# The dense part's first four products, parts of x and two weight conversions moved among the attention's last transposes

## The chip, the core and the metric

The kernel runs on one core of one Trainium2 chip. The metric is the device time of one execution in microseconds (us). The kernel before took 1040.09 us, the median of three runs (1038.75, 1040.09 and 1040.95).

## What is computed

Three parts follow each other. The attention keeps, in each row of scores, only those within `tau` of the row's largest, and its output, with the heads side by side, is the input x of the first feed-forward part, whose output is the input of the second.

```python
# q, k, v: (4, 8, 576, 64); tau = 0.02
scores = 1.0 / np.sqrt(64) * np.matmul(q, k.transpose(0, 1, 3, 2))
thresh = np.max(scores, axis=-1, keepdims=True) - tau
scores = np.where(scores >= thresh, scores, -1000000000.0)
scores = scores - np.max(scores, axis=-1, keepdims=True)
attn = np.exp(scores)
attn = attn / (np.sum(attn, axis=-1, keepdims=True) + 1e-09)
x = np.matmul(attn, v)             # then (2304, 512): rows batch and token
# first feed-forward part: w_in (512, 2048), w_out (2048, 512), alpha (2048,)
h = x @ w_in
g = np.maximum(h, 0.0) + alpha * np.minimum(h, 0.0)
x = g @ w_out
# second: w1, w2 (512, 1024), w3 (1024, 1024), w_out2 (1024, 512)
out = ((x @ w1) * (x @ w2) @ w3) @ w_out2
```

## The kernel before

**The attention** goes through 16 pairs of heads. A pair has nine score units (four chunks of 128 rows for each of two heads, and one chunk that holds the last 64 rows of both). Each unit runs through a row of steps with names that the kernel's table of turns uses, with the unit's number behind the letter:

- Q, scores on TensorE (PE, line 402) into one of three PSUM slots; R, row maximum on VectorE (DVE, L426); H, threshold (DVE, L429); E, exponential on ScalarE (ACT, L437); M, masking with the row sum (DVE, L451), after which the PSUM slot is free.
- G, a small guard on GpSimd (POOL, L462); I, reciprocal (DVE, L467); C, scaling of the row (POOL, L474).
- T, transposes of the scaled rows on PE (L491, in three groups of four or five per chunk); X, their eviction by ACT (L501 to L509).
- V, the product with v (PE, L518, one for each half of the rows) and Y, its eviction by ACT into `xT` (L531, L533).

Ahead of a pair stand the loads of q and k (a), their splits into a high and a low part on POOL (bq0hi, bq0lo and so on, L181 and L188) and their transposes (PE, L291). The order of all these steps is fixed by `turn_order`: it emits a step as soon as what it depends on has been emitted, in the order of `PER * P + AT[key]`, with P the pair and `AT` a table of numbers. Each engine then works through its own queue in that order, and so does SyncE (SP), which issues the DMAs. Between the pairs, the first 14 tiles of w_in are loaded and converted (w0 to w8).

**The first feed-forward part** (the dense part) computes `h = x @ w_in` in three passes: x and the weights are split into a high and a low part of about half the bits, and of the four products of parts three are made. For a tile of 512 tokens one h product is 12 matmuls of 128x512 (PE, L985, out `h`), 16 of them (f = 0 to 15) cover the 2048 columns. ACT and DVE make g from h (L1056, L1061), then split it into `gs` (L183, L188), and an acc product of 12 matmuls (L985, out `acc`) adds its part of `g @ w_out` in four PSUM banks. The numbers f of the acc products follow those of the h products some places behind. Before the first h product stand the splits of x: four high parts on ACT (L183, `x<-xT`) and four low parts on DVE (L188).

**The conversions.** w_out, and the last two tiles of w_in, come as 64-bit numbers. A tile of them is loaded by SP into one of two buffers `raw` (L794); ACT makes two parts of it (L196 `raw<-raw` and L202 `m<-raw`), DVE does three steps on one part (L207, L209, L213), POOL adds the two (L218, `m<-m,raw`), which frees the `raw` buffer for the next load. ACT and DVE make the high and low half of the weights from the sum (`wu`, L823 and L829). The low half needs `sign_sb`, which DVE makes in three instructions (L760 to L762).

The order of the dense part is set by `list_order`, a planner that goes by costs in the code and hands out the buffers (`raw` 2, `m` 3, `u` 2, `gs` 2, `h` 4 banks). It begins where the attention's list ends, and all attention buffers are closed between the two:

```python
        for o in turn_order(ops, slots):
            o.emit(*o.engines)
...
        att_ctx.close()
...
        for o in list_order(ops, slots, DENSE_TURN):
            o.emit(o.engine)
```

The second feed-forward part follows in the same list.

## Time and profile before

| what | value |
|---|---|
| median of three runs | 1040.09 us |
| the profiled execution | 1039.72 us |
| span of the profile (first to last instruction) | 1037.9 us |
| PE busy | 1014.1 us (98%) |
| VectorE busy | 751.6 us (72%) |
| ScalarE busy | 580.6 us (56%) |
| GpSimd busy | 340.1 us (33%) |
| mean granted clock of PE | 0.998 of full speed |
| last attention product with v begins | 303.64 us after the span's start |
| first h product, first acc product | 307.66 us, 317.57 us |
| first dense tile's last h product begins | 385.48 us |

Times within the span count from its first instruction. The profiled execution took 1.82 us more than its span, and 0.37 us less than the median of the runs. A row of a timeline has start, length, engine, line, operation, output and inputs, shapes and number of instructions; in brackets stand the idle time of the engine before it and what ended that. The end of a matmul is modelled and holds its latency, so a group's length is more than the distance to the next group.

### The profile page before, as it was taken

Reading aid. Unit: us, or ns where it says so; the run is one execution under the profiler, and the core shown is the slowest. Engines: PE = TensorE matmul, PEld = TensorE weight load, DVE = VectorE, ACT = ScalarE, POOL = GpSimd, SP = SyncE. Lnnn points to the kernel's source line nnn. Section 1 sums busy time; section 2 is a strip of 40 time slices with the busy share of each in tenths; the row PEclk is TensorE's granted clock in tenths of the full one; section 3 lists DMA queues with packets and bytes.
Section 4 is the critical chain, followed back from the end, with each engine's and each line's share of the span. In section 5 each row is a group of like instructions: output and inputs, shape, how many; then the busy total and the mean of one; then the engine's idle time right before and its main releaser. Section 6 shows DMA issues by size and latency. Waiting matters only on the chain.

```text
span 1037.9 us, 16931 instructions
## 1 busy us (share of the span) xinstructions
PE 1014.1 (98%) x5870; PEld 867.0 (84%) x5870; DVE 751.6 (72%) x1556; ACT 580.6 (56%) x1119; POOL 340.1 (33%) x469
## 2 busy tenths in 40 slices
PE   8999999999989999999999999999999999999997
PEld 6778777777858889988888888888899999999997
DVE  7999999999858787667656565638475587577554
ACT  5998989999865665544443344324143363345331
POOL 4888888888733232222211211103200000000000
PEclk9999999999999999999999999999999999999999
DMA  5353443435113333434524233512242233224201
GB/s 128 90 141 100 131 112 117 125 89 153 39 41 104 112 110 114 141 117 156 176 80 142 104 136 106 172 41 72 92 139 75 81 108 122 71 72 148 91 11 61
DMA packets 71445, 109.50 MB, mean 106 GB/s; under 512 B 14912, under 2 KB 43584, under 8 KB 71360
## 3 DMA queue, kind: packets, MB, share of 16 engines
q1 hardware_dynamic: 68992, 108.16, 33.3%
q8 instruction: 46, 0.75, 0.3%
q10 hardware_dynamic: 2368, 0.27, 0.2%
q14 instruction: 39, 0.32, 0.1%
HBM read 80.22 MB, written 18.35 MB: 95 GB/s over the span
## 4 chain that ended last, share of the span: by engine, by line
PE 87%; POOL 5%; issue 2%; DVE 2%; ACT 2%; DMA 1%; SPq 0%; POOLq 0%; ACTq 0%; DVEq 0%
PE h L985 25%; PE acc L985 24%; PE h L1341 17%; PE pv_ps L518 8%; PE pt_ps L491 5%; PE s_ps L402 5%; POOL p L474 3%; PE tr L291 2%; POOL ks L181 1%; POOL qs L181 1%; PE zero L352 1%; PE h L858 1%; DMA raw<-in_moe_w_dram 0%; POOL praw L474 0%; ACT qT L311 0%
## 5 line engine op out<-in xcount | busy, mean ns | idle before, releaser
L985 PE MATMUL h<-x,wa 128*128 128x512 f32 (+1 forms) x960 | 212.4, 371 | 1.1 <-ACT x L183 1.1
L985 PE MATMUL acc<-gs,wu 128*128 128x512 f32 (+1 forms) x960 | 209.8, 368 | 0.4 <-DVE wu L829 0.4
L985 PEld LDWEIGHTS h<-x,wa 128*128 128x128 f32 x960 | 167.3, 189 | 32.6 <-ACT x L183 3.0
L985 PEld LDWEIGHTS acc<-gs,wu 128*128 128x128 f32 x960 | 168.1, 189 | 31.0 <-DVE wu L829 0.8
L1341 PE MATMUL h<-T,sw 128*128 128x384 f32 x1008 | 190.6, 336 | 0.0
L1341 PEld LDWEIGHTS h<-T,sw 128*128 128x128 f32 x1008 | 178.4, 188 | 8.3
L218 POOL TENSOR_TENSOR m<-m,raw 128x512 int32<-128x512 int32 x58 | 81.6, 1408 | 281.5 <-DVE m L213 213.9
L1405 DVE TENSOR_TENSOR ct<-h,ct 128x384 f32<-128x384 f32 x120 | 66.8, 557 | 91.6 <-PE h L1341 91.5
L426 DVE TENSOR_REDUCE sm<-s_ps 128x1 f32<-128x576 f32 x144 | 105.6, 751 | 13.2 <-PE s_ps L402 13.1
L437 ACT ACTIVATE e<-s_ps,sm 128x576 f32<-128x576 f32 x144 | 106.0, 764 | 7.4 <-DVE sm L426 4.7
L474 POOL TENSOR_SCALAR p<-p,sm 128x576 f32<-128x576 f32 x128 | 96.7, 762 | 26.8 <-DVE sm L467 17.7
L451 DVE SCALAR_TENSOR_TENSOR p<-s_ps,sm,e 128x576 f32<-128x576 f32 x128 | 102.6, 811 | 0.8 <-ACT e L437 0.8
L183 ACT CAST gs<-g 128x512 fp32r<-128x512 f32 (+1 forms) x80 | 46.2, 577 | 94.2 <-PE acc L985 77.5
L491 PE MATMUL pt_ps<-ident,p 128*128 128x128 f32 x576 | 87.3, 280 | 11.3 <-ACT pt L505 8.7
L188 DVE TENSOR_TENSOR gs<-g,gs 128x512 fp32r<-128x512 f32 (+1 forms) x80 | 60.0, 750 | 47.0 <-ACT gs L183 46.4
L1056 ACT ACTIVATE g<-h,sign_sb 128x512 f32<-128x512 f32 (+1 forms) x80 | 51.3, 642 | 69.5 <-PE h L985 62.2
L1061 DVE SCALAR_TENSOR_TENSOR g<-h,salpha_sb,g 128x512 f32<-128x512 f32 (+1 forms) x80 | 55.6, 694 | 47.3 <-ACT g L1056 47.2
L491 PEld LDWEIGHTS pt_ps<-ident,p 128*128 128x128 f32 x576 | 66.0, 142 | 26.5 <-POOL praw L474 10.5
L518 PE MATMUL pv_ps<-pt,vraw 128*64 128x256 f32 (+1 forms) x640 | 84.7, 411 | 0.3 <-ACT xT L531 0.2
L183 ACT CAST sw<-w 128x512 fp32r<-128x512 f32 (+1 forms) x96 | 54.0, 569 | 55.4 <-PE h L1341 53.6
L505 ACT COPY pt<-pt_ps 128x512 f32<-128x512 f32 x128 | 74.5, 596 | 15.6 <-PE pt_ps L491 14.6
L985 PE MATMUL acc<-wp,x 128*128 128x512 f32 x288 | 81.9, 394 | 0.0
(121 smaller groups left out, 1521.3 us busy)
## 6 DMA issues: line engine op xcount, KB each, us to landing
raw<-in_moe_w_dram SPq DMA_DIRECT2D x32, 512.0 KB, 3.7
raw<-in_moe_w_out_dram SPq DMA_DIRECT2D x24, 512.0 KB, 3.5
w<-w SPq DMA_DIRECT2D x48, 256.0 KB, 2.6
qU<-qT SPq DMA_DIRECT2D x30, 320.0 KB, 4.0
w<-w SPq DMA_DIRECT2D x24, 384.0 KB, 2.9
wraw<-in_moe_w_in_dram SPq DMA_DIRECT2D x14, 512.0 KB, 3.8
w<-m SPq DMA_DIRECT2D x24, 256.0 KB, 2.1
z<-w SPq DMA_DIRECT2D x24, 256.0 KB, 2.7
```

Source lines behind the costliest of these rows:

```text
L183: eng.copy(out=dst, in_=src)
L218: nc.gpsimd.tensor_tensor(out=mc[0], in0=mc[0], in1=mc[1], op=ALU.add)
L426: nc.vector.tensor_reduce(out=sm_of(u, 0), in_=st[u], axis=AX.XY, op=ALU.max, negate=True)
L437: nc.scalar.activation(out=es[u].rearrange("p (j s) -> p j s", j=2), in_=st[u], func=AF.Exp, bias=sm_of(u, 0))
L451: nc.vector.scalar_tensor_tensor(out=p_at(u).rearrange("p (j s) -> p j s", j=2), in0=st.pop(u), scalar=sm_of(u, 1), in1=es.pop(u).rearrang ...
L474: nc.gpsimd.tensor_scalar(out=out, in0=in_, scalar1=sm_of(u, 3), scalar2=1.0, op0=ALU.mult, op1=ALU.mult)
L491: nc.tensor.transpose(t[:, i, :], p[:, at + i * 128 : at + (i + 1) * 128], ident)
L505: nc.scalar.copy(out=pt[:, g, 0:4, to], in_=ps)
L518: nc.tensor.matmul(out=o[64 * hh : 64 * hh + 64, 0:n], lhsT=vr[:, hh, i, :], rhs=pt[:, 0 if i == 4 and not half else hh, i, :], start=(i = ...
L985: nc.tensor.matmul(out=out, lhsT=l, rhs=r, start=first and i == 0, stop=last and i == n - 1)
L1341: nc.tensor.matmul(out=bank_()[:, 0:HT], lhsT=w()[:, ap_, kc * 128 : kc * 128 + 128], rhs=x()[:, bp, kc * HT : kc * HT + HT], start=first ...
L1405: lambda e: ENG[e].tensor_tensor(out=dst(), in0=x(), in1=y(), op=how),
```

## The change

The last attention pair (15) gets its own numbers in the table of turns (keys that end in `_L`), and steps of the first dense tile become steps of the attention's list, so that the table sets their place too: the four splits of x (zx0h to zx3l), the first four h products (zh0 to zh3) with what ACT and DVE make of them (zu, zg; for the first two also the splits za, zb), and the first two conversions of w_out (zw00 to zw16). The four early h products write PSUM slots of the scores (`h_early`, two products to a slot of two banks) in place of the `h` banks. The attention's buffers close in three steps: those of the splits and loads first (`narrow`), then those of q and k (`narrower`, with the three sign instructions), then the rest, at the end of the list. The arithmetic is the same. `list_order` still plans the whole dense part; the steps that have been emitted are left out where its list is emitted.

```diff
+class Late:
+    def __init__(self):
+        self.pools = {}
+
+    def open(self, pool, *tags):
+        for t in tags or (None,):
+            self.pools[t] = pool
+
+    def tile(self, *args, tag=None, **kw):
+        return self.pools.get(tag, self.pools.get(None)).tile(*args, tag=tag, **kw)
...
-        att = att_ctx.enter_context(tc.tile_pool(name="att", bufs=1, side="right"))
+        long_ctx, mid_ctx, short_ctx = ExitStack(), ExitStack(), ExitStack()
+        att_long = long_ctx.enter_context(tc.tile_pool(name="att_long", bufs=1))
+        att_mid = mid_ctx.enter_context(tc.tile_pool(name="att_mid", bufs=1))
+        att = short_ctx.enter_context(tc.tile_pool(name="att", bufs=1))
...
+        def att_op(key, P, engine, emit, deps=(), take=None, free=()):
+            own = key + ("_0" if not P else "_L" if P == NPAIR - 1 else "")
+            at = AT[own if own in AT else key]
+            o = Op({engine: 0.0}, emit, PER * P + at, deps, take, free)
+            o.key = key, P
+            att_ops.append(o)
+            named[key, P] = o
+            return o
...
-        for o in turn_order(ops, slots):
-            o.emit(*o.engines)
...
-        att_ctx.close()
...
+        EARLY = 4
+        early_banks = {}
+
+        def early_bank(f):
+            def get():
+                if f - f % 2 not in early_banks:
+                    early_banks[f - f % 2] = ps_a.tile([128, 2, 512], F32, tag="s", name="h_early", bufs=3)
+                return early_banks[f - f % 2][:, f % 2]
+
+            return get
...
+        def narrow(e):
+            short_ctx.close()
+            front = ctx.enter_context(tc.tile_pool(name="front", bufs=2, side="right", reuse_waits="tile"))
+            dn.open(front, "x", "u")
+
+        def narrower(e):
+            mid_ctx.close()
+            dn.open(ctx.enter_context(tc.tile_pool(name="dn", bufs=2, side="right", reuse_waits="tile")))
...
+        t1 = att_op("zs", LP, "S", narrow, users_short)
+        t2 = att_op("zt", LP, "S", narrower, users_mid + [t1])
+        begun[t1], begun[t2] = t1, t2
+        x_parts = []
+        for kc, (h, l) in enumerate(first_x):
+            early(f"zx{kc}h", h, "A", [t1])
+            early(f"zx{kc}l", l, "V", [h])
+            x_parts += [h, l]
+        for f in range(2):
+            ld, c, m0, m1, m2, m3, a = w_out_steps[f]
+            early(f"zw{f}0", ld, "S", [t2])
+            early(f"zw{f}1", c, "A", [ld])
+            early(f"zw{f}2", m0, "A", [ld])
+            for i, (m, before) in enumerate(((m1, m0), (m2, m1), (m3, m2))):
+                early(f"zw{f}{3 + i}", m, "V", [before])
+            early(f"zw{f}6", a, "P", [c, m3])
+        for f in range(EARLY):
+            hj, u, g, h, l = first_jobs[f]
+            early(f"zh{f}", hj, "T", x_parts, take=None if f % 2 else "s")
+            early(f"zu{f}", u, "A", [hj], take="zu")
+            early(f"zg{f}", g, "V", [u], free=[first_jobs[f - f % 2][0]])
+            if f < 2:
+                early(f"za{f}", h, "A", [g, t2])
+                early(f"zb{f}", l, "V", [h], free=[u])
+        for o in turn_order(att_ops, {"s": 3, "e": NEB, "ptp": 2, "pt": 2, "m": 1, "p": NPB, "praw": 1, "zu": 2}):
+            o.emit(*o.engines)
+
+        att_ctx.close()
+        long_ctx.close()
...
         for o in list_order(ops, slots, DENSE_TURN):
-            o.emit(o.engine)
+            if o not in begun:
+                o.emit(o.engine)
```

The new pools also move tiles of the attention: `kT`, `qT`, `qU` and `swap` to `att_mid`; v's raw tiles, `sm`, `e`, `p`, `praw` and `pt` to `att_long`.

What this does to the queues is confined to the last pair and the first dense tile; ahead of the last pair's first splits and behind the first dense tile the order is the same on every engine. Three places matter below. In the rows that follow the lines of the changed kernel are up to some 20 higher (L491 is L506, L985 is L993, L451 is L466).

PE, from the last scores to the first acc product, before:

```order
L402 MATMUL s_ps<-kT,qU 128x288 x2
L491 MATMUL pt_ps<-ident,p 128x128 x10
L491 MATMUL pt_ps<-ident,praw 128x128 x5
L491 MATMUL pt_ps<-ident,p 128x128 x17
L518 MATMUL pv_ps<-pt,vraw_104 64x256 x10
L491 MATMUL pt_ps<-ident,p 128x128
L518 MATMUL pv_ps<-pt,vraw_104 64x320 x10
L985 MATMUL h<-x,wa 128x512 x36
L985 MATMUL acc_4748<-gs,wu_4720 128x512 x2
```

The same place in the changed kernel:

```order
L417 MATMUL s_ps<-kT,qU 128x288 x2
L506 MATMUL pt_ps<-ident,p 128x128 x5
L993 MATMUL h_early<-x,wa 128x512 x24
L506 MATMUL pt_ps<-ident,p 128x128 x9
L993 MATMUL h_early<-x,wa 128x512 x12
L506 MATMUL pt_ps<-ident,p 128x128 x5
L993 MATMUL h_early<-x,wa 128x512 x12
L506 MATMUL pt_ps<-ident,p 128x128 x4
L533 MATMUL pv_ps<-pt,vraw_110 64x320 x10
L533 MATMUL pv_ps<-pt,vraw_110 64x256 x10
L993 MATMUL h<-x,wa 128x512 x12
L993 MATMUL acc_4790<-gs,wu_4767 128x512 x2
```

Four h products stand between the last 23 transposes, and a fifth stands ahead of the first acc product. The first early product writes the slot of the last scores, so it waits for the last mask.

DVE, the last masks of the attention (L451) and what follows, before:

```order
L426 TENSOR_REDUCE sm<-s_ps 128x1
L451 SCALAR_TENSOR_TENSOR p,sm<-s_ps,sm,e 128x576
L429 TENSOR_SCALAR sm<-sm,ctau 128x1
L451 SCALAR_TENSOR_TENSOR p,sm<-s_ps,sm,e 128x576
L467 RECIPROCAL sm<-sm 128x2
L760 TENSOR_SCALAR sign_sb<-alpha_sb 128x16
L761 TENSOR_SCALAR sign_sb<-sign_sb 128x16
L762 TENSOR_TENSOR salpha_sb<-sign_sb,alpha_sb 128x16
L188 TENSOR_TENSOR x<-xT_71,x 128x512 x4
```

The same engine in the changed kernel (one more low part of x stands some ten rows further ahead):

```order
L200 TENSOR_TENSOR x<-xT_71,x 128x512 x2
L444 TENSOR_SCALAR sm<-sm,ctau 128x1
L482 RECIPROCAL sm<-sm 128x1
L466 SCALAR_TENSOR_TENSOR p,sm<-s_ps,sm,e 128x576 x2
L482 RECIPROCAL sm<-sm 128x2
L1541 TENSOR_SCALAR sign_sb<-alpha_sb 128x16
L1544 TENSOR_SCALAR sign_sb<-sign_sb 128x16
L1545 TENSOR_TENSOR salpha_sb<-sign_sb,alpha_sb 128x16
L200 TENSOR_TENSOR x<-xT_71,x 128x512
L441 TENSOR_REDUCE sm<-s_ps 128x1
```

All four low parts of x and the three sign instructions come ahead of the last three row maxima and masks.

ACT, from the last evictions of transposes (L505, in the changed kernel L520) to the first weight's high half. Before:

```order
L183 CAST x<-xT_71 128x512 x4
L196 ACTIVATE raw<-raw 128x512
L202 ACTIVATE m<-raw 128x512
L196 ACTIVATE raw<-raw 128x512
L202 ACTIVATE m<-raw 128x512
L1056 ACTIVATE g<-h,sign_sb 128x512
L183 CAST gs<-g 128x512
L823 ACTIVATE wu_4720<-m,sign_sb 128x512
```

In the changed kernel:

```order
L1080 ACTIVATE g<-h_early,sign_sb 128x512
L520 COPY pt<-pt_ps 128x4x128
L214 ACTIVATE m<-raw 128x512
L208 ACTIVATE raw<-raw 128x512
L214 ACTIVATE m<-raw 128x512
L546 COPY xT_74<-pv_ps 128x256
L548 COPY xT_75<-pv_ps 128x64
L208 ACTIVATE raw<-raw 128x512
L1080 ACTIVATE g<-h_early,sign_sb 128x512
L195 CAST gs<-g 128x512
L1080 ACTIVATE g<-h_early,sign_sb 128x512
L546 COPY xT_74<-pv_ps 128x256
```

ACT begins the conversions behind the eviction of the last transposes, and the eviction of the first product with v stands between their parts.

On POOL six splits of the last pair stand ahead of two scales of pair 13 (C1 and C4), where two of them stood. On SP two loads of w_out stand ahead of the three loads of v for the last pair; the first of the two waits for scores of pair 14, the second for the last scores of pair 15. Near the end of the first dense tile the sixteenth h product stands one acc product later than before; ahead of the fifteenth acc product all 16 h products and 14 acc products have been made in both kernels.

## Rows read from the trace of the kernel before

**Rows 1.** The page, busy time of PE, share of the span, and the other engines.

```profile
PE 1014.1 (98%) x5870; PEld 867.0 (84%) x5870; DVE 751.6 (72%) x1556; ACT 580.6 (56%) x1119; POOL 340.1 (33%) x469
```

**Rows 2.** Timeline of PE from 290 to 326: start, length, line, operation.

```profile
294.52 0.74 PE L491 MATMUL pt_ps<-ident,p 128*128 128x128 f32 x5 [0.81 <-ACT pt L505]
295.59 0.74 PE L491 MATMUL pt_ps<-ident,praw 128*128 128x128 f32 x5 [0.34 <-ACT pt L509]
296.94 3.75 PE L491 MATMUL pt_ps<-ident,p 128*128 128x128 f32 x17 [0.61 <-POOL sm L462]
...
307.66 9.34 PE L985 MATMUL h<-x,wa 128*128 128x512 f32 x36 [1.10 <-ACT x L183]
...
317.57 2.79 PE L985 MATMUL acc<-gs,wu 128*128 128x512 f32 x11 [0.35 <-DVE wu L829]
```

**Rows 3.** Stretches: length, busy time of PE, PEld, DVE, ACT, POOL; clock, DMA, GB/s.

```profile
293.50:297.00 3.50, 1.75 (x13) 1.18 (x11) 2.78 (x10) 3.18 (x8) 1.89 (x4) 0.98 0.03 7
297.00:300.60 3.60, 3.60 (x17) 3.08 (x17) 0.45 (x1) 1.91 (x5) 1.15 (x2) 0.54 0.00 0
...
307.00:317.00 10.00, 9.29 (x37) 6.87 (x37) 8.98 (x13) 6.92 (x13) 3.02 (x2) 1.00 0.22 72
...
326.00:394.00 68.00, 68.00 (x301) 55.85 (x299) 55.62 (x83) 40.43 (x69) 22.96 (x16) 1.00 0.34 116
```

**Rows 4.** Timeline of VectorE from 286 to 300.

```profile
292.23 0.76 DVE L426 TENSOR_REDUCE sm<-s_ps 128x1 f32<-128x576 f32 x1 [1.22 <-PE s_ps L402]
...
295.21 0.82 DVE L451 SCALAR_TENSOR_TENSOR p<-s_ps,sm,e 128x576 f32<-128x576 f32 x1 [0.33 <-ACT e L437]
...
296.83 0.62 DVE L762 TENSOR_TENSOR salpha_sb<-sign_sb,alpha_sb 128x16 f32<-128x16 f32 x1
```

**Rows 5.** Timeline of VectorE from 305 to 330.

```profile
307.64 2.50 DVE L188 TENSOR_TENSOR x<-xT,x 128x512 fp32r<-128x512 f32 x4 [10.18 <-ACT x L183]
...
315.73 1.78 DVE L829 SCALAR_TENSOR_TENSOR wu<-m,sign_sb,wu 128x512 fp32r<-128x512 f32 x1
...
318.10 0.74 DVE L829 SCALAR_TENSOR_TENSOR wu<-m,sign_sb,wu 128x512 fp32r<-128x512 f32 x1
```

**Rows 6.** Timeline of ACT from 293 to 330, two first steps of conversions.

```profile
309.06 0.69 ACT L196 ACTIVATE raw<-raw 128x512 int32<-128x512 uint32 x1
...
320.76 0.69 ACT L196 ACTIVATE raw<-raw 128x512 int32<-128x512 uint32 x1 [0.22 <-DMA raw<-in_moe_w_out_dram]
```

**Rows 7.** Timeline of POOL, additions of the conversions, 300 to 336 and 340 to 396.

```profile
312.18 1.30 POOL L218 TENSOR_TENSOR m<-m,raw 128x512 int32<-128x512 int32 x1 [14.02 <-DVE m L213]
315.25 1.72 POOL L218 TENSOR_TENSOR m<-m,raw 128x512 int32<-128x512 int32 x1 [1.77 <-ACT gs L183]
...
340.88 1.30 POOL L218 TENSOR_TENSOR m<-m,raw 128x512 int32<-128x512 int32 x1 [4.80 <-DVE m L213]
...
349.62 1.31 POOL L218 TENSOR_TENSOR m<-m,raw 128x512 int32<-128x512 int32 x1 [4.43 <-DVE m L213]
...
390.55 1.60 POOL L218 TENSOR_TENSOR m<-m,raw 128x512 int32<-128x512 int32 x1 [1.99 <-DVE m L213]
```

**Rows 8.** Timelines of PE and of VectorE at the end of the first dense tile.

```profile
388.20 5.75 PE L985 MATMUL acc<-gs,wu 128*128 128x512 f32 x24
...
390.23 0.75 DVE L829 SCALAR_TENSOR_TENSOR wu<-m,sign_sb,wu 128x512 fp32r<-128x512 f32 x1
```

**Rows 9.** Timeline of POOL from 254 to 266: a split, and a scale.

```profile
255.26 0.64 POOL L181 TENSOR_SCALAR qs<-qraw 128x256 fp32r<-128x256 f32 x1 [0.36 <-POOL p L474]
...
256.76 0.74 POOL L474 TENSOR_SCALAR p<-p,sm 128x576 f32<-128x576 f32 x1
```

**Rows 10.** Timeline of PE from 254 to 279, the transposes behind that scale.

```profile
258.27 0.60 PE L491 MATMUL pt_ps<-ident,p 128*128 128x128 f32 x4
```

**Rows 11.** The page, DMA issues: KB each, median us from issue to landing.

```profile
raw<-in_moe_w_out_dram SPq DMA_DIRECT2D x24, 512.0 KB, 3.5
```

**Rows 12.** Waits of ACT from 317 to 394: us in total, times, longest.

```profile
ACT raw L196 <- DMA raw<-in_moe_w_out_dram: 7.2, 7, 2.3
```

More of the change, by code (lines that the diff above doesn't have):

```diff
@@ L496, in trans_ev @@
             if (P, half) not in pts:
-                pts[P, half] = att.tile([128, 2, 5, 256 + ST * half], F32, tag=f"pt{half}", name="pt")
+                pts[P, half] = att_long.tile([128, 2, 5, 256 + ST * half], F32, tag=f"pt{half}", name="pt")
             pt = pts[P, half]
@@ L563, in lo_w_in @@
             split_lo(ENG[e], dst[:, 1], wa.pop(("x", f)), dst[:, 0])
-        ops = []
-        def op(key, P, engine, emit, deps=(), take=None, free=()):
-            at = AT[key + "_0" if not P and key + "_0" in AT else key]
-            ops.append(Op({engine: 0.0}, emit, PER * P + at, deps, take, free))
-            named[key, P] = ops[-1]
-            return ops[-1]
+        att_ops = []
+        def att_op(key, P, engine, emit, deps=(), take=None, free=()):
[6 more added lines that the diff above has]
+            return o
@@ L1040 @@
             xs, xl = split_x(t, now - 3, [])
+            if t == order[0]:
+                first_x = xl
             acc = [bank(f"acc{m}", bufs=1) for m in range(KD)]
             for f in range(NF):
-                ps, gt, gs = bank("h"), lazily(lambda: dn.tile([128, 512], F32, tag="u", name="g")), part_pair("gs")
+                begins = t == order[0] and f < EARLY
+                ps, gt, gs = early_bank(f) if begins else bank("h"), lazily(lambda: dn.tile([128, 512], F32, tag="u", name="g")), part_pair("gs")
                 hj = op(
@@ new lines, with early, emit @@
+        LP = NPAIR - 1
+        users_mid = [o for o in att_ops if o.key[0][0] == "Q" and o.key[1] >= NPAIR - 2]
+        users_short = [o for o in att_ops if o.key[0][0] in "cwb" and o.key[1] >= NPAIR - 3]
+        begun = {}
+        def early(key, o, engine, deps, take=None, free=()):
+            def emit(e):
+                o.emit(e)
+            begun[o] = att_op(key, LP, engine, emit, [begun[d] for d in deps], take, [begun[d] for d in free])
+            o.engines, o.prio, o.wait, o.bias = {engine: 0.01}, o.prio - 1000, {}, 0.0
```

87 lines of the change are left out of this document (48 added, 39 removed).

## The prediction

> **What bounds the kernel now.** I read the page first: TensorE (PE) is busy for 1014.1 us, 98% of the span [rows 1], so a change can only pay where PE stands still, or where it lets PE stand still. Next I read PE's timeline around the place that the change touches, the end of the last attention pair and the first products of the dense part. There PE waits 0.81, 0.34 and 0.61 us for evictions and for a row sum, then 1.10 us for the first x part and 0.35 us for the first w_out tile [rows 2]. The table of stretches adds the clock: from 293.5 to 297 PE is busy for 1.75 of 3.5 us, and from 297 to 300.6 the granted clock is 0.54, which is mostly the lower of its two levels (1.2 GHz, against 2.4) [rows 3]. With 3.6 us at about half speed this costs some 1.7 us. From 326 to 394 PE is busy throughout: 301 matmuls in 68.0 us, which is 25 products of twelve at 2.72 us each [rows 3]. So whatever PE gains before that shows at the end, unless a later wait takes it back.
>
> That later wait is the point of this prediction. Sixteen w_out tiles and the last two w_in tiles are converted during the first dense tile: 18 POOL additions in nine pairs, the first at 312.18, the last at 390.55 [rows 7]. They go through two `raw` buffers, and a load starts only when an addition has released a buffer; it lands 3.5 us after its issue [rows 11]. ACT waits for loads of w_out seven times in all, for 7.2 us [rows 12]; the first of these is at 320.76 [rows 6]. At the far end the low half of tile 14's weights is done at 390.23 + 0.75 = 390.98, and PE reaches that product at 388.20 + 2.72 = 390.92, needing the low half one matmul (0.23 us) later [rows 8]. PE has no idle time there and no margin either. **The first dense tile is bounded by PE and by the chain of conversions at once.**
>
> **The change, part by part.** (1) *The last pair's q and k splits on POOL.* Six of them now stand ahead of two scales of pair 13 where two stood. Two splits took 256.76 - 255.26 = 1.50 us [rows 9], so four more take at most 3.0 us; the added ones are mostly the shorter hi copies and I take 2.0. The scale ended at 257.50, its transposes began at 258.27 [rows 9, 10]: 0.77 us of slack, so PE is 1.2 us later there, at most 2.2, at least nothing. PE's small waits behind take some of it; I carry 1.0.
>
> (2) *x's splits and the signs.* They leave the stretch in which PE waits: ACT's four hi copies, after which ACT converts from 309.06 [rows 6], and VectorE's four lo parts (2.50 us) [rows 5]. PE's idle 1.10 us goes [rows 2]. But on VectorE the four lo parts and the three sign instructions (0.62 us for the longest [rows 4]; 1.0 for all) now stand ahead of the last row maxima and masks. The last mask ended at 295.21 + 0.82 = 296.03, with 1.22 and 0.33 us of idle time before it [rows 4]. Now it ends at 296.0 + 2.5 + 1.0 - 1.55 + 1.0 (from 1) = 299.0.
>
> (3) *Four early products.* The first of them writes the bank that the last mask reads, so it begins at 299.0. Of PE's work before that stretch [rows 2] the scores and two groups of transposes still stand ahead of it; I estimate that they are done at about 296. So one wait of some 3 us replaces 0.81, 0.34 and 0.61; whether the clock falls, as it did after the sparse stretch [rows 3], decides 1.7 us. From there PE is full: four products (10.9 us) and 18 transposes of about 0.1 us (4 began at 258.27 and lasted 0.60 with their latency [rows 10]; 1.9 us) end at 311.8. The two attention products and a fifth h product follow without a wait.
>
> (4) *Two conversions.* Their loads now stand ahead of the last v loads on SP and wait for the last scores; v is needed some 13 us after those, against 3.5 us for a load, so this costs nothing. But ACT's part stands behind the last transposes' eviction, at about 312.7, where it was 309.06 before [rows 6]. Before, the two additions ended 4.4 and 7.9 us after that start (313.48 and 316.97 [rows 7]). VectorE has no gate work between the two now, so I take 3.3 and 5.8 (and keep 4.4 and 7.9 as the other end): 316.0 and 318.5. The first acc product needs, after that, two gates, a low part and the first weight's low half (0.74 + 0.69 + 0.74 + 0.75 us): it starts at about 320.7 with five h products done. Before, acc began at 317.57 with three done [rows 2]; with two more, 317.57 + 2 x 2.72 = 323.0. **PE is 2.3 us ahead at this point**, 0.6 if the clock falls.
>
> (5) *What is late next.* The additions are later: 316.0 for 313.48 and 318.5 for 316.97. The loads into their buffers land at 319.5 and 322.0. The third conversion's load was there by 313.48 + 3.5 = 317.0 before, yet ACT, which had other work in line, came to it only shortly before the fourth's 320.76; so it loses about 0.5, and the fourth, which waited for its load, 1.2 [rows 6]. If the clock falls, both lose 1.7 more. From there the chain runs by itself: nine pairs, from 315.25 to 390.55 in eight rounds of 9.41 us. PE, with 25 products to go, is at tile 14 at 320.7 + 68.0 = 388.7, and waits for it until about 391.0 plus the chain's loss. So **the 2.3 us are given back at the fifteenth tile**, and the chain's own delay remains: 0.9 us without the fall of the clock, 2.6 with it. Rounds are not all alike: the shortest is 349.62 - 340.88 = 8.74 us [rows 7], so with fewer waits in line some delay is made up (at most 8 x 0.67 = 5.4 us). I take +1.0 us.
>
> The profiled execution took 1039.72 us, 1.82 more than its span and 0.37 below the median of the runs (1040.09). The sum is 1039.72 + 1.0 = **1040.7 us**. From the second dense tile on the order of the instructions is the same, and what is gained or lost stays.
>
> **A rule against the change.** A low half made while POOL added took 1.78 us, the next one without it 0.74 [rows 5]; POOL's addition lasted from 315.25 to 316.97 [rows 7]. The lo parts of x are moved among POOL's scales of 0.74 us [rows 9], where no row shows how the two get on. If three of them wait for one scale each, the last mask is 2.2 us later, and so are the early products and conversions. The Trainium skill (SBUF — State Buffer, Who interferes with whom) states it so: an instruction of VectorE with both inputs in SBUF contends with one of GpSimd that reads there, and whichever issues second is blocked until the first is done. By that rule the sum would be nearer 1042.9; the low half above agrees with it [rows 5].
>
> **The rivals.** *Faster: the chain keeps pace.* If its rounds come nearer 8.74 us than 9.41, because the gates in line before its steps now come earlier, PE's 2.3 us stay, and more where the wait for the last mask is short: PE would start acc no later than all its work allows, and the idle time named above plus the slow clock (1.76 + 1.10 + 0.35 + 1.7 = 4.9 us) could go. That gives 1035 to 1037.5, say 1036. For it: every addition has idle time before it, so no engine is full. Against it: in the change the first two conversions start later, and loads, not engines, set a round.
>
> *Slower: the low clock.* The wait for the last mask empties PE for 3 us in one piece. If the products behind it run at 1.2 GHz for as long as the transposes did (3.6 us), conversions start 1.7 us later and tile 14 is 2.6 us late, or 4 with the other end of (4): 1042.3 to 1043.7, say 1043. It decides once the second addition ends some 3 us later than the 316.97 of before, at 320 or after. For it: the row of 0.54 follows a stretch that was half busy. Against it: 1.10 us of idle time before 307.66 did not lower the clock of what followed, 1.00 from 307 to 317 [rows 2, 3].
>
> *Slower: VectorE and POOL in each other's way*, as worked out above: about 1042.9.
>
> *No effect*: the early products wait so long that they fill nothing. Then PE comes to acc as before and the chain sets the end; this falls within the forecast.
>
> **How the numbers follow.** A measurement of this kernel tells about 0.2% (2.1 us) from no change. Forecast, within 1038.0 and 1042.2: 0.42. The chain keeps pace: 0.27. The low clock: 0.22. VectorE against POOL: 0.09. So faster 0.27, same 0.42, slower 0.31. The likeliest case alone spans 1039 to 1042. The range takes in most of the rivals, without the best of the first and the worst of the second: 1035.0 to 1044.0.
>
> **What would show it.** PE should wait some 3 us for a mask of VectorE before the first early product; with the low clock behind it the second rival is in play. The first two additions should end near 316.0 and 318.5 (on this axis), acc should start near 320.7, and PE should wait 2 to 3 us for a low half of weights at the last tiles. If PE has no such wait at the end of the first dense tile, the step on the chain is wrong and the kernel is faster; if x's lo parts last 1.4 us and not 0.6, the rule on the shared access holds there. The prediction falls altogether if acc starts later than 323.

## The result, and the profile after

The changed kernel took 1046.12 us, the median of six runs (1045.0 to 1048.39); the kernel before took 1040.07 us beside it, also the median of six. The ratio is 1.0063, with an interval of 1.005 to 1.0076: slower by 6 us, above the predicted 1040.7 and outside the range. The profiled execution took 1046.95 us, its span is 1045.2 us, 7.3 more than before. The changed kernel's executions differ from each other more than those of before, and the longer ones show a lower mean granted clock of PE: 1045.0 us at 0.997, 1048.39 at 0.994 (the profiled execution of before: 0.998).

The page first. PE is busy for 2.9 us more than in [rows 1], with the same 5870 matmuls, so some of them ran longer:

```profile
PE 1017.0 (97%) x5870; PEld 868.3 (83%) x5870; DVE 753.4 (72%) x1557; ACT 580.5 (56%) x1118; POOL 340.8 (33%) x469
```

The timeline of PE in the changed kernel, at the place of [rows 2] (L506 are the transposes, L993 the products):

```profile
296.64 0.76 PE L506 MATMUL pt_ps<-ident,p 128*128 128x128 f32 x5
300.37 8.49 PE L993 MATMUL h_early<-x,wa 128*128 128x512 f32 x24 [2.96 <-DVE p L466]
...
316.50 5.07 PE L533 MATMUL pv_ps<-pt,vraw 128*64 128x320 f32 x40
...
325.79 0.50 PE L993 MATMUL acc<-gs,wu 128*128 128x512 f32 x1 [1.27 <-ACT wu L831]
326.58 4.37 PE L993 MATMUL acc<-gs,wu 128*128 128x512 f32 x11 [0.28 <-DVE wu L837]
330.78 2.88 PE L993 MATMUL h<-x,wa 128*128 128x512 f32 x12
```

One wait of 2.96 us for a mask, as forecast, and behind it 24 matmuls in 8.49 us. Then a second wait, which was not forecast: 1.27 and 0.28 us for the two halves of the first w_out weights, and behind that 11 matmuls in 4.37 us, where before took 2.79 for 11 [rows 2]. The table of stretches, with the columns of [rows 3], says why both are long:

```profile
300.30:306.30 6.00, 5.93 (x14) 4.71 (x15) 1.79 (x6) 0.00 (x0) 3.32 (x6) 0.50 0.03 8
...
326.50:330.80 4.30, 4.22 (x12) 3.33 (x13) 2.57 (x6) 2.12 (x4) 1.36 (x1) 0.60 0.01 5
```

The granted clock is 0.50, its lower level (1.2 GHz), for 6 us behind the first wait, and 0.60 on average for 4.3 us behind the second. At the other level (2.4 GHz) the 24 matmuls take 5.64 us (the run with ten zeros in two pieces, below), so in the profiled execution the first fall cost 8.49 - 5.64 = 2.85 us, the second 4.37 - 2.79 = 1.6.

Where the two kernels have done as many products, two rows of before tell the loss so far (timeline of PE, before):

```profile
325.64 2.88 PE L985 MATMUL h<-x,wa 128*128 128x512 f32 x12
...
393.83 5.28 PE L985 MATMUL h<-x,wa 128*128 128x256 f32 x36
```

The first stands against 330.78 above: 5.1 us later. The second holds the first three products of the second tile, and in the changed kernel they begin at 401.93, 8.1 us later (timeline of PE):

```profile
397.92 0.49 PE L993 MATMUL acc<-gs,wu 128*128 128x512 f32 x1 [1.05 <-ACT wu L831]
399.30 2.79 PE L993 MATMUL acc<-gs,wu 128*128 128x512 f32 x11 [0.89 <-DVE wu L837]
401.93 4.48 PE L993 MATMUL h<-x,wa 128*128 128x256 f32 x36
```

So the chain of conversions is late at the fifteenth tile, by 1.05 + 0.89 us. Of the 8.1 us, 0.8 come back at once: the 36 matmuls take 5.28 us in the kernel before and 4.48 in the changed one, at a clock of 1.00 in both, and the 7.3 us that are left are those of the span. Why the kernel before is slower there is not shown; its profile has no wait in that place, but VectorE still makes parts of x for this tile until 395.69.

Last, the waits of PE from 250 to 410 (total us, times, longest), in the changed kernel and then in the kernel before:

```profile
PE h_early L993 <- DVE p L466: 3.0, 1, 3.0
PE acc L993 <- ACT wu L831: 2.3, 2, 1.3
PE pt_ps L506 <- POOL p L489: 1.6, 2, 1.4
PE acc L993 <- DVE wu L837: 1.2, 2, 0.9
PE pt_ps L506 <- ACT pt L520: 0.6, 2, 0.3
PE h L993 <- POOL wa L200: 0.3, 1, 0.3
```

```profile
PE pt_ps L491 <- ACT pt L505: 1.6, 3, 0.8
PE h L985 <- ACT x L183: 1.1, 1, 1.1
PE pt_ps L491 <- POOL sm L462: 0.6, 1, 0.6
PE acc L985 <- DVE wu L829: 0.4, 1, 0.4
PE pt_ps L491 <- ACT pt L509: 0.3, 1, 0.3
PE pv_ps L518 <- ACT xT L531: 0.2, 1, 0.2
```

Together 9.0 us now and 4.2 before. With the slow clock, 2.85 + 1.6 = 4.45 us now against the 1.7 of before, PE lost 13.45 us there and 5.9 before. The difference, 7.55, is the 7.3 us of the span to within 0.3, which is in part luck: the sum leaves out the 0.8 us just named, and the recorded waits fall short of what PE lost (at the last tiles 0.34 + 1.05 + 0.89 = 2.3 us, while the delay grew from 5.1 to 8.1). What it does show is that **the change took waits away and made larger ones.**

### The profile page after: what moved, and what is told of

It reads as the page before. It is cut to its first block, busy times and chain, and to the rows that moved or that the text cites. A ratio compares the mean times of both kernels' runs of the same rounds, so it can differ in the third digit from the quotient of the medians.

```text
span 1045.2 us, 16886 instructions
## 1 busy us (share of the span) xinstructions
PE 1017.0 (97%) x5870; PEld 868.3 (83%) x5870; DVE 753.4 (72%) x1557; ACT 580.5 (56%) x1118; POOL 340.8 (33%) x469
## 4 chain that ended last, share of the span: by engine, by line
PE 82%; POOL 6%; DVE 3%; DMA 3%; issue 2%; ACT 2%; SPq 0%; POOLq 0%; ACTq 0%; DVEq 0%
PE h L993 23%; PE acc L993 22%; PE h L1367 17%; PE pv_ps L533 6%; PE s_ps L417 5%; PE pt_ps L506 5%; POOL p L489 3%; PE tr L306 2%; PE h_early L993 1%; POOL m L230 1%; POOL ks L193 1%; DMA raw<-in_moe_w_out_dram 1%; POOL qs L193 1%; DVE m L219 1%; PE zero L367 1%
## 5 line engine op out<-in xcount | busy, mean ns | idle before, releaser
L993 PE MATMUL acc<-gs,wu 128*128 128x512 f32 (+1 forms) x960 | 211.5, 371 | 3.5 <-ACT wu L831 2.3
L993 PE MATMUL h<-x,wa 128*128 128x512 f32 (+1 forms) x912 | 199.9, 369 | 0.3 <-POOL wa L200 0.3
L993 PEld LDWEIGHTS acc<-gs,wu 128*128 128x128 f32 x960 | 169.3, 190 | 35.2 <-ACT wu L831 3.2
L993 PEld LDWEIGHTS h<-x,wa 128*128 128x128 f32 x912 | 158.0, 189 | 28.7 <-POOL wa L200 0.8
L466 DVE SCALAR_TENSOR_TENSOR p<-s_ps,sm,e 128x576 f32<-128x576 f32 x128 | 102.6, 811 | 2.0 <-ACT e L452 1.9
L506 PE MATMUL pt_ps<-ident,p 128*128 128x128 f32 x576 | 86.3, 277 | 10.9 <-ACT pt L520 7.1
L1080 ACT ACTIVATE g<-h,sign_sb 128x512 f32<-128x512 f32 (+1 forms) x76 | 48.6, 641 | 74.6 <-PE h L993 61.7
L506 PEld LDWEIGHTS pt_ps<-ident,p 128*128 128x128 f32 x576 | 64.7, 140 | 26.5 <-POOL praw L489 10.3
L1085 DVE SCALAR_TENSOR_TENSOR g<-h,salpha_sb,g 128x512 f32<-128x512 f32 (+1 forms) x76 | 52.6, 692 | 46.3 <-ACT g L1080 46.3
L520 ACT COPY pt<-pt_ps 128x512 f32<-128x512 f32 x128 | 74.6, 595 | 17.1 <-PE pt_ps L506 15.7
L993 PE MATMUL acc<-wp,x 128*128 128x512 f32 x288 | 81.9, 395 | 0.0
```

Source lines behind the costliest of these rows:

```text
L466: nc.vector.scalar_tensor_tensor(out=p_at(u).rearrange("p (j s) -> p j s", j=2), in0=st.pop(u), scalar=sm_of(u, 1), in1=es.pop(u).rearrang ...
L506: nc.tensor.transpose(t[:, i, :], p[:, at + i * 128 : at + (i + 1) * 128], ident)
L520: nc.scalar.copy(out=pt[:, g, 0:4, to], in_=ps)
L993: nc.tensor.matmul(out=out, lhsT=l, rhs=r, start=first and i == 0, stop=last and i == n - 1)
```

## The experiments

Each run changes the changed kernel, and its ratio is to the kernel before, on the same chip (1039.2 to 1039.5 us there). In seven runs the emitted list is altered behind `turn_order` by a small helper: `behind("A", "B", "C")` puts the last pair's steps B and C right behind its step A. A difference in us between two runs is that of their ratios.

**The splits on POOL.** The last pair's loads and splits of q and k go back to their places (ten numbers leave the table):

```diff
-'aq_L': 95.62, 'bq0hi_L': -79.761, 'bq0lo_L': 89.381, 'bq1hi_L': -82.87, 'bq1lo_L': 106.425,
-'ak_L': 95.5, 'bk0hi_L': -66.749, 'bk0lo_L': -82.88, 'bk1hi_L': -99.57, 'bk1lo_L': 109.699
```

> The changed kernel with the last pair's q and k loads and splits in the order of before (their own numbers in the table taken out); nothing else moves. Theory A (the end of the first dense tile is set by the chain of conversions, which begins behind the eviction of the last transposes; whatever delays that eviction delays everything): PE's 1.43 us wait for a POOL scale at 259.86 goes, all behind it is 1.4 us earlier, the early products begin near 298.9 instead of 300.37 and the kernel takes about 1044.7 us (1.4 less than the changed kernel's 1046.1). Rival B (the splits' delay is taken up by later waits of the attention): 1046.1, with the early products still at 300.4.

1043.85 us, ratio 1.0047 (1.0033 to 1.006). That is 1.7 us less than the change (0.0016 in the ratio), but the two intervals overlap, so the trace has to carry it:

```profile
299.64 7.35 PE L993 MATMUL h_early<-x,wa 128*128 128x512 f32 x24 [2.96 <-DVE p L466]
```

PE's wait of 1.43 us for the scale is gone, but the first early product began only 0.73 us earlier than 300.37, and its wait is 2.96 us as before. The span of this profile is 0.7 us shorter than the change's (1044.5 for 1045.2), so the trace carries 0.7 of the 1.7 us. Half of the delay of the scale had been taken up by small waits behind it, as step (1) had it.

**Two conversions far ahead.** The loads go ahead of v, ACT's, VectorE's and POOL's parts into the stretch where these engines stand idle:

```diff
+        behind("zt", "zw00", "zw10", "v")
+        behind("E3", "zw02", "zw01", "zw12", "zw11")
+        behind("I3", "zw03", "zw04", "zw05", "zw13", "zw14", "zw15")
+        behind("C2", "zw06", "zw16")
```

> The changed kernel with the two early conversions further ahead: ACT's four steps directly behind the last exponentials, VectorE's six behind the last reciprocal, POOL's two additions behind the last scale. PE's order and the wait of 3 us for the last mask stay. Theory A: additions end near 306 and 308 instead of 321.1 and 323.5, PE no longer waits ahead of the first acc product (1.27 and 0.28 us, and the fall of the clock behind them, some 1.8 us), and the waits of 1.05 and 0.89 us at the fifteenth acc product shrink: about 1042.5 us. Rival C (the time is lost on PE alone, in the wait for the mask and the low clock of 300 to 306): the waits ahead of acc go, 1.5 us, but the rest stays: 1044.5.

1044.45 us, ratio 1.0049 (1.0036 to 1.0061), the number of the rival, and 1.5 us less than the change, with overlapping intervals. The additions start at 305.87 and 308.45, some 14 us earlier; the wait of 1.27 us before acc is gone, and with it the second fall of the clock. But the fifteenth tile still waits for 1.0 + 0.9 us. ACT and POOL in this run show why:

```profile
324.24 1.34 ACT L831 ACTIVATE wu<-m,sign_sb 128x512 fp32r<-128x512 f32 x2
325.48 0.67 ACT L208 ACTIVATE raw<-raw 128x512 int32<-128x512 uint32 x1
```

```profile
328.48 1.37 POOL L230 TENSOR_TENSOR m<-m,raw 128x512 int32<-128x512 int32 x1 [18.73 <-DVE m L225]
```

The third conversion stands behind the first two weights in ACT's queue, and their place is set by g and PE. Its addition comes at 328.48, where the change has 329.26. The early start of two is lost at the third.

**Three conversions far ahead.** To the four lines of the run above come three, and the third conversion takes the buffer that the first leaves:

```diff
-        for f in range(2):
+        for f in range(3):
...
+        behind("zw16", "zw20")
+        behind("zu0", "zw22", "zw21")
+        behind("zb0", "zw23", "zw24", "zw25", "zw26")
```

> The changed kernel with three conversions of w_out (one more) in the early part, and all three far ahead: ACT's steps directly behind the last exponentials and behind the first early gate. The wait of 2.96 us and the order of PE up to the first acc product stay. Theory A (the chain of conversions sets the end of the first dense tile): the chain is one conversion ahead, so that PE has no wait at the fifteenth acc product (1.01 and 0.88 us with two early conversions) and none ahead of the first one; 2 to 3 us less than with two, about 1.003 of the kernel before. Rival (the order that the planner gives to ACT and VectorE holds the chain, not its start): the waits at the fifteenth acc product stay near 1.9 us, 1.005.

1042.63 us, ratio 1.0029 (1.0018 to 1.0041), the number of the theory and 3.5 us less than the change, with the intervals apart. The third addition starts at 315.88. PE's waits from 250 to 410 in this run:

```profile
PE h_early L993 <- DVE p L466: 3.0, 1, 3.0
PE pt_ps L506 <- POOL p L489: 2.3, 2, 2.1
PE h L993 <- DVE wa L200: 1.7, 2, 1.1
...
```

Both waits for w_out weights at the fifteenth tile are gone; what is late now is the low part of w_in's last two tiles, 1.7 us. So the chain does set that place, through its order on ACT.

**VectorE's queue.** To see whether it holds the mask back, the low parts of x go to POOL, and the three sign instructions, here a step of their own (`zq`), behind the last masks:

```diff
-            early(f"zx{kc}l", l, "V", [h])
+            early(f"zx{kc}l", l, "P", [h])
...
+        behind("G5", "zx0l")
+        behind("C5", "zx3l")
+        behind("C8", "zx2l")
+        behind("I3", "zq")
```

> The changed kernel with the four low parts of x made by POOL instead of VectorE, and the three sign instructions behind the last masks. VectorE's queue loses 3.5 us ahead of the last masks. Theory A: the first early product begins near 297 instead of 300.37, PE's wait for the mask shrinks from 2.96 us to below 1, the clock does not fall, so that the last early transposes end near 310 instead of 315.97, and the kernel takes about 1040.5 us. Rival D (VectorE and POOL block each other, or POOL is late with the low parts): the masks are hardly earlier, the first early product waits for POOL, at 299 or later; 1044 or more.

1049.13 us, ratio 1.0094 (1.0081 to 1.0108): worse. VectorE in this run, ahead of the mask:

```profile
294.96 0.17 DVE L482 RECIPROCAL sm<-sm 128x2 f32<-128x2 f32 x1 [2.83 <-POOL sm L477]
...
297.32 0.76 DVE L441 TENSOR_REDUCE sm<-s_ps 128x1 f32<-128x576 f32 x1 [1.29 <-PE s_ps L417]
...
299.82 0.82 DVE L466 SCALAR_TENSOR_TENSOR p<-s_ps,sm,e 128x576 f32<-128x576 f32 x1 [0.58 <-ACT e L452]
```

VectorE stands idle for 2.83, 1.29 and 0.58 us, and PE's wait is 2.96 us again. So VectorE's queue is not what PE waits for; the mask waits for ACT. The rival had the outcome, neither forecast the cause. Why the run is worse is only in part shown: POOL has the low parts ahead of scales, and PE waits 0.68 us for one, but the span of the profile is only 1.0 us longer than the change's, where the ratio makes 3.2. The clock is 0.992 to 0.996 in its four executions, 0.994 to 0.997 in the change's six.

**The path of the mask.** In the changed kernel, ACT and VectorE between PE's last transposes (296.64 to 297.40) and the first early product:

```profile
297.33 0.58 ACT L520 COPY pt<-pt_ps 128x512 f32<-128x512 f32 x1 [0.62 <-PE pt_ps L506]
297.82 0.27 ACT L522 COPY pt<-pt_ps 128x128 f32<-128x128 f32 x1
297.97 2.02 ACT L452 ACTIVATE e<-s_ps,sm 128x576 f32<-128x576 f32 x3
```

```profile
299.39 0.82 DVE L466 SCALAR_TENSOR_TENSOR p<-s_ps,sm,e 128x576 f32<-128x576 f32 x1 [0.67 <-ACT e L452]
```

ACT evicts PE's own last transposes, then makes the exponentials; the mask takes the second of them, and PE waits for the mask, which ends at 300.21. VectorE had made the row maxima and thresholds of all three units by 298.71. It is a loop that starts at PE and has a fixed length: whatever moves PE's transposes moves the wait, but does not shorten it. That is why it is 2.96 us in the changed kernel and in four of the runs. Two runs cut the loop: the row maxima, exponentials and masks of the units 2 and 3 go ahead of unit 7's, and the exponentials ahead of ACT's last evictions, so that the mask that frees the bank comes earlier. The first of the two:

```diff
+        behind("I1", "R2", "H2", "R3", "H3", "E2", "zx1l")
+        behind("X10", "E3", "M2", "M3", "G3")
+        behind("R7", "I3", "C3", "C2")
+        behind("I7", "zq")
```

> The changed kernel with the maxima, exponentials and masks of the units 2 and 3 of the last pair (their scores are ready 7 us before) moved ahead of those of unit 7, on ACT ahead of the evictions of the last transposes, and the signs behind the last reciprocal. PE's order is the same; the bank of the first early product is now freed by the mask of unit 2. Theory A2 (PE's wait of 2.96 us is a fixed path that starts at PE's own transposes: two evictions on ACT, the exponential, the mask; what stands in VectorE's queue ahead of them does not matter): the path is cut, the first early product begins within 1 us of the end of the transposes before it, the clock does not fall there, the last early transposes end near 310.5 instead of 315.97; the kernel is 3.5 to 5.5 us faster than the changed one, that is 1.001 to 1.003 of the kernel before on the same chip (the changed one is at 1.0063). Rival C2 (another operand holds the product, the low parts of x or the slot): the wait stays above 2 us and the time is as in the changed kernel.

1044.94 us, ratio 1.0054 (1.0041 to 1.0067). PE's wait for the mask is gone, but it waits 3.35 us for a scale on POOL instead, since the edit put the guard G3, which needs the later masks, ahead of that scale (POOL in this run):

```profile
298.96 0.19 POOL L477 TENSOR_SCALAR sm<-sm 128x2 f32<-128x2 f32 x1 [3.53 <-DVE p L466]
299.24 2.19 POOL L489 TENSOR_SCALAR p<-p,sm 128x576 f32<-128x576 f32 x3
```

The gap is longer than the old one, and the clock is at 0.50 behind it here too, with another engine at its end. With the guard behind the scale (against the run above):

```diff
-        behind("X10", "E3", "M2", "M3", "G3")
-        behind("R7", "I3", "C3", "C2")
+        behind("X10", "E3", "M2", "M3")
+        behind("H7", "I3", "C3", "C2")
+        behind("C1", "G3")
```

> The masks again, with the guard behind the last pair's scale on GpSimd, so that GpSimd's order is that of the change. Theory (the wait for the mask is a closed path from PE's own last transposes, and the slow clock is the price of any one long gap there): no wait of 3 us is left before the first early product, at most 1.5 us; the clock stays at 1.00 from 300 to 306 in the profile; early products begin near 299, the last transposes near 312.5; the conversions' chain still bounds the end, so only part of the 3 to 4 us shows: ratio 0.998 to 1.002 without the chain, 1.002 to 1.004 with it. Rival (the clock falls wherever early products follow transposes, gap or not): clock at half speed again and a ratio of 1.005, as in the run of the masks before.

1042.41 us, ratio 1.0029 (1.0018 to 1.0039), 3.5 us less than the change and within what the theory gave with the chain. PE in this run:

```profile
297.68 5.74 PE L993 MATMUL h_early<-x,wa 128*128 128x512 f32 x24
...
320.66 0.49 PE L993 MATMUL acc<-gs,wu 128*128 128x512 f32 x1 [1.27 <-ACT wu L831]
321.45 4.38 PE L993 MATMUL acc<-gs,wu 128*128 128x512 f32 x11 [0.29 <-DVE wu L837]
```

No gap of 3 us, the clock at 1.00 from 293 to 308, the early products 2.7 us earlier and at full speed. So the loop through ACT is what PE waited for. This run also tells which bank it was. The first early product begins at 297.68, right behind the mask of unit 2 (296.80 to 297.62) and ahead of those of units 3 (297.91) and 7 (300.28). It is thus the bank of unit 2, the third from last to get its scores, and not the slot of the last scores, as the description of the change has it; in the changed kernel PE waits for the first of the last three masks, not for the last. The waits for the conversions are untouched, and so is the fall of the clock behind the first of them.

**The clock alone.** Ten matmuls of zeros, on no data of the kernel, fill a part of the gap of 2.96 us:

```diff
+        z = att_op("z1", LP, "T", lambda e: multiply_zeros(5), [named["T12", LP]], take="ptp")
...
+        z = att_op("z2", LP, "T", lambda e: multiply_zeros(5), [z], take="ptp")
```

> The changed kernel with ten matmuls on zeros ahead of the first early product, as before in one piece of ten, now in two pieces of five that use both slots of the transposes, so that the fifth h product gets the same bank as in the changed kernel (that with one piece of ten waited 3.61 us for the eviction of the last attention product, which the changed kernel does not do). Results of the zeros are not used. If the fall of the clock behind the wait is what costs about 3 us, and it does not fall where PE is kept busy: granted clock near 1.00 from 300 to 306, no wait of 3.6 us ahead of the fifth h product, 2 to 3 us less than the changed kernel, about 1.004 of the kernel before. Rival: the clock falls in part of the executions all the same, or the time goes to a later wait for the conversions; 1.006 to 1.009.

1045.07 us, ratio 1.0059 (1.0047 to 1.0071). In the profiled execution the early products begin 0.5 us later than in the change and run at full speed:

```profile
298.46 2.57 PE L367 MATMUL zero<-zeros 128*128 128x512 f32 x10 [0.56 <-ACT pt L520]
300.87 5.64 PE L993 MATMUL h_early<-x,wa 128*128 128x512 f32 x24
```

Its mean clock is 1.000, and the eleven matmuls of the fifteenth tile that stood at 399.30 in the change begin 3.1 us earlier, at 396.16. But the median of six gains only 0.4 us in the ratio, and the other executions have 0.995 to 0.999. Nor does this profile alone show that the zeros kept the clock up, for in the run with three early conversions it stayed at 1.00 behind the same gap left empty. The profiles together show more. Seven have a gap of about 3 us in this place (the change, the splits, two and three early conversions, the low parts on POOL, the first run of the masks, the first with all three); in six of them the clock from 300 to 306 is 0.50 to 0.82, in one 1.00. Four have no such gap (both with zeros, the second of the masks, the last below), and all four have 1.00. So the fall goes with the gap, though not each time; what it costs in the median no run here isolates.

The same with the ten zeros in one PSUM slot:

> The changed kernel with ten more matmuls on zeros (128x512, results not used) on PE directly ahead of the first early product, in the place where PE waits for the last mask. They take 2.3 us and fill most of the 2.96 us wait. If the wait's emptiness lowers the clock (theory A's part on the clock): granted clock stays at 1.00 from 300 to 306, the four early products and the transposes between them end about 3 us earlier (last early transposes near 313.0 instead of 315.97), conversions begin 3 us earlier and the kernel takes about 1043 us. Rival: the clock falls anyway, or the zeros delay the first product; 1046 or slightly more.

1048.01 us, ratio 1.0085 (1.0071 to 1.0099). One slot more shifted the turn of the banks: the fifth h product got the bank of the last attention product, whose eviction on ACT stands behind gates (the steps that make g from h), and PE waited 3.61 us for it, until 323.12. Its clock is 1.00 from 300 to 306, and behind that wait too; its time tells of the banks.

**All three together**: the splits back, the masks moved (with the guard still ahead of the scale), three early conversions (the first two now behind steps of unit 7, which are the last in this order).

> All that the other runs do apart, in one: the last pair's splits in the order of before, the masks of the units 2 and 3 ahead of that of unit 7, three conversions far ahead. Theory A with A2: PE's idle time of the stretch from 293 to 317 is nearly gone, the first early product begins near 296, acc near 317 with five h products done (323.0 would be equal to the kernel before), and no wait for conversions is left at the end of the first dense tile: about 0.995 of the kernel before, 5 us faster. Rival: a further wait (the last scales on POOL, the first product with v, the eviction ahead of acc) takes part of it: 0.998 to 1.000.

1041.04 us, ratio 1.0021 (1.0012 to 1.0031), slower than both forecasts. The wait of 3.35 us for POOL stands in it too, with a clock of 0.62 from 299.5 to 303, and PE waits 1.8 us for w_in at the last tiles. With the guard behind the scale:

> The three changes together (order of the last pair's splits, masks moved, three early conversions), with the guard behind the scale. Theory: the wait of 3.35 us for GpSimd is gone, the first early product starts near 297.5 (299.55 in the run without this), acc begins near 320.5 with five h products done; the two waits for the low part of w_in near 1.2 and 0.7 us stay, as they come from the conversions behind. Ratio 0.998 to 1.000. Rival (the end of the first dense tile is set by the conversions alone, whatever PE does before): 1.002 as before, with the waits for weights longer by what PE gained.

**1038.62 us, ratio 0.999 (0.9981 to 0.9999), eleven runs against seventeen**: 7.6 us less than the change, and by the interval a little faster than the kernel before (0.8 us between the medians, less than the 2.1 us from which on the prediction counts a difference). It is what the theory had. PE in this run, and its waits from 250 to 410:

```profile
296.80 5.78 PE L993 MATMUL h_early<-x,wa 128*128 128x512 f32 x24
...
319.80 2.79 PE L993 MATMUL acc<-gs,wu 128*128 128x512 f32 x11 [0.34 <-DVE wu L837]
...
392.81 4.47 PE L993 MATMUL h<-x,wa 128*128 128x256 f32 x36
```

```profile
PE h L993 <- DVE wa L200: 1.8, 2, 1.2
PE pt_ps L506 <- ACT pt L520: 1.1, 3, 0.6
PE pt_ps L506 <- POOL p L489: 0.5, 2, 0.3
PE acc L993 <- DVE wu L837: 0.3, 1, 0.3
```

The first eleven acc matmuls begin at 319.80 with five h products done, 3.2 us ahead of the 323.0 that the prediction worked out for before. The second tile begins at 392.81, 1.0 us ahead of 393.83: of the 3.2 us, 1.8 went into the waits for w_in at the last tiles, so the chain still bounds that place. The waits sum to 3.7 us and no stretch from 294 to 394 has a lower clock; against the 5.9 us of before that makes 2.2 us, and the span is 2.0 shorter. The profiled execution is the fastest of the eleven, so this is more than the 0.8 us of the medians. All eleven executions have a mean clock of 0.999 or 1.000. By the ratios the three changes are worth 1.7 (of which the trace carries 0.7), 3.5 and 3.5 us alone, and 7.6 together.

This account, waits and slow clock from 250 to 410, gives the span's change to within 0.3 us in the change, the second run of the masks and the last run, with the same luck; in the other runs it can be off by over 1 us (all three with the guard ahead: 2.4 by the account, 1.1 measured).

## Why the prediction was wrong, point by point

**The splits, step (1).** PE's transposes behind the scale were 1.6 us later (259.86, where [rows 10] have 258.27), inside the bounds of 0 and 2.2; I carried 1.0, and the run with the splits back gives 0.7 at the early products. The six splits lasted from 254.87 to 259.06, 4.2 us, which is 2.7 more than the two of before [rows 9]; I had taken 2.0.

**The mask, steps (2) and (3).** The wait came out at 2.96 us, for "some 3 us", by luck: both its ends were 1.4 us later than I had them (the transposes ended at 297.40 for 296, the products began at 300.37 for 299.0), and the cause was wrong. I added x's parts and the signs to VectorE's queue and had the last mask end at 299.0; in the trace VectorE is through with them, and with the three row maxima behind them, at 298.71 and waits 0.67 us for ACT. The order of ACT, two evictions ahead of three exponentials, was in the difference of the orders but not in my working. Nor was it the last mask: that one ends at 302.15, 1.8 us after the products began.

**The clock, step (3), is the term that failed most.** "Whether the clock falls decides 1.7 us": I named it, put it at 0.22 and left it out of the sum. In the profiled execution it fell, for 6 us and not 3.6, and cost 2.85. Against it I held that an idle 1.10 us before 307.66 had not lowered it [rows 2, 3]; that row was no match for a gap of 3 us. With the later start, 1.37 us, and 0.2 each for the transposes and for the other two early products, the two attention products began at 316.50, where I had 311.8: 4.7 us late.

**The conversions, step (4).** Everything behind follows by the steps. ACT began at 317.22 for 312.7; POOL's additions:

```profile
319.78 1.29 POOL L230 TENSOR_TENSOR m<-m,raw 128x512 int32<-128x512 int32 x1 [15.34 <-DVE m L225]
322.22 1.32 POOL L230 TENSOR_TENSOR m<-m,raw 128x512 int32<-128x512 int32 x1 [1.14 <-issue]
```

They ended at 321.07 and 323.54, that is 3.85 and 6.3 us after ACT's start (I took 3.3 and 5.8; the other ends were 4.4 and 7.9). Acc's first matmul began at 325.79, the eleven that need the low half at 326.58, for 320.7: 3.6 us behind the 323.0 of before, not 2.3 ahead. The text said that it falls if acc begins later than 323.

Two slips of the working stand here. The four terms behind the second addition sum to 2.92 us (the trace has 326.58 - 323.54 = 3.04), which from 318.5 gives 321.4 and not 320.7, so the lead was at most 1.6 us. And I named no wait of PE before acc, although my own numbers hold one: 311.8, the two attention products (5.0 us in the trace) and the fifth h product (2.72) come to 319.5, 1.2 us ahead of 320.7. So the sum had no second fall of the clock, which cost 1.6 us more.

**The chain, step (5).** The mechanism held: PE waited for weights at the fifteenth tile, 1.94 us (2 to 3 were forecast, for the low half alone; 1.05 of it was for the high half), and three early conversions took that away. What it was late by was mis-sized, +1.0 for what became 8.1, because it inherits steps (3) and (4). That shorter rounds make up some of a delay did not hold. The last addition of the nine pairs:

```profile
398.72 1.69 POOL L230 TENSOR_TENSOR m<-m,raw 128x512 int32<-128x512 int32 x1 [1.61 <-ACT x L195]
```

It ended at 400.41, 8.3 us after the 392.15 of before [rows 7], and the second addition had been 6.6 late (323.54 against 316.97): the chain lost 1.7 us more on the way, it made up nothing.

**The rivals.** "The low clock" is what happened, with its sign and its point of decision (the second addition ended at 323.54, past 320), at 1043 for 1046. Its price lacked the second fall, a fall longer than that of [rows 3], and the later start of the early products. "VectorE and POOL in each other's way" is there, and small. Beside POOL's scale the two low parts took 1.78 us, where four took 2.50 [rows 5], that is about 0.5 more:

```profile
290.52 1.78 DVE L200 TENSOR_TENSOR x<-xT,x 128x512 fp32r<-128x512 f32 x2
```

```profile
290.42 0.74 POOL L489 TENSOR_SCALAR p<-p,sm 128x576 f32<-128x576 f32 x1
```

The Trainium skill (SBUF — State Buffer, Who interferes with whom) has the one that issues second blocked until the first is done, which agrees with these two rows, once: the scale runs until 291.16, 0.64 us past the start of the low parts. The 2.2 us that I gave the rival were for three such blocks. "The chain keeps pace" did not happen; even with three early conversions and the other two changes the ratio is 0.999, short of the 0.995 to 0.9975 that its 1035 to 1037.5 us are.

## What to carry to other kernels

When work is moved into a stretch of waits, follow the wait that it makes around the whole loop, through every queue that it passes, to its start; if the loop starts at the engine that waits, adding or removing work elsewhere does not shorten it, and only another order of the loop does. Price a gap of the matrix engine at its own length and once more at the slow clock that may follow it (from nothing to 2.85 us here), and look at each place where a later step can open a second gap. A start that is brought forward is only worth what the next item in the same queue can follow: two early conversions brought 1.5 us by the ratio, three 3.5.

## What the runs showed of the hardware

The clock did not answer the same gap alike. Behind the same 2.96 us the 24 matmuls took 8.49 us in the changed kernel's profile, 7.35 in that of the splits, and 5.73 in that of the three early conversions (clock 1.00 from 300 to 306; timeline of PE):

```profile
300.88 5.73 PE L993 MATMUL h_early<-x,wa 128*128 128x512 f32 x24 [2.96 <-DVE p L466]
```

The wait of 3.61 us in the run with the zeros in one slot was not followed by a lower clock either. One kernel's executions spread accordingly: with the three early conversions 1040.3 and 1041.1 us at a mean clock of 0.999, and 1042.59 to 1044.03 at 0.996 or 0.997. And a wait of 1.27 us with 0.28 behind it was followed by the lower clock in the changed kernel (4.37 us for 11 matmuls) and in the second run of the masks (4.38), but not in the run with the zeros in two pieces (2.80) nor in the first run of the masks (2.80). In this last one the lower clock came at the fifteenth tile instead, behind waits of 1.01 and 0.88 us (4.37). So one profile does not tell what a gap costs in the median; the last kernel, which has neither gap, has the least spread of all, 1.3 us over eleven executions against 3.4 over six of the change.
